# Scores of 16 of 24 attention pairs: stacked full-height matmuls in place of row-tiled ones, and one output tile fewer

## Chip, cores and metric

One core of one Trainium2 chip. The metric is the device time of one launch in microseconds; lower is better. The kernel before took 720.41 us (median of three runs, 712.51 to 721.36).

## What is computed

Softcapped attention over 4 batches of 12 heads, 448 positions of 64 features, and on its output, seen as 1792 tokens of 768 features, a two-layer network with the nonlinearity h - tanh(h). All in float32.

```python
scores = np.matmul(q, k.transpose(0, 1, 3, 2)) / np.sqrt(64)
scores = cap * np.tanh(scores / cap)
attn = softmax(scores)                       # over the last axis, 1e-9 in the denominator
x = np.matmul(attn, v).transpose(0, 2, 1, 3).reshape(4 * 448, 12 * 64)
h = x @ w_in                                 # 768 -> 2048
out = (h - np.tanh(h)) @ w_out               # 2048 -> 768
```

The kernel reads w_in and w_out as 64-bit words and decodes them on the chip.

## The kernel before

**Precision.** TensorE's fast format keeps fewer bits than float32. So most operands are split: a "hi" part, the value rounded by a cast to that format, and a "lo" part, the rest (`split`, L438: a cast on ACT or DVE, L432 or L434, then a subtraction on DVE, L443). A product takes three matmuls: hi by hi, hi by lo, lo by hi.

**Pairs.** Attention goes by pairs (b, p): two heads of a batch, one on partitions 0 to 63, the other on 64 to 127. There are 24 pairs, six a batch. `prep_pair` (L525) transposes the raw k and q to [128, 448] tiles kT and qT (L536), splits k into kst (hi in the first half of the columns, lo in the second), copies the tails of both heads into kt (L550, two copies of 64x128 in a tile whose other blocks are zero), and makes the hi and lo parts of q in qst (L557 on ACT, L562 on DVE).

**Scores.** `scores` (L668) runs four groups for a pair. The first is the tail: the last 64 keys of both heads as one 128-row block, three matmuls from kt. The other three take 128 keys of both heads: six matmuls on 64 rows each, alternating between the two heads and so between the two halves of the array's rows, into two PSUM banks (L616 in `qk_group`, L599). The bank tag "s" has two buffers; pairs 0 to 7 also use the accumulators' banks (`s_banks`, `FREE_PAIRS = 8`). ACT then takes tanh out of the bank (L626) and exp (L681). The products with v follow (`pv`, L742): eleven pairs in plain float32 (L760), thirteen in split form (L762, L763, L765), whose exponentials are split as well (L664, L657).

**Network.** `moe` (L1160) goes through segments (batch, first and last of 16 blocks of 128 hidden features): `first` (L1074, matmuls L1089 to L1091, 18 of 384 columns) gives h for a block, ACT and DVE make and split g, and `second` (L1120, L1142) adds its part to the output accumulators, three tiles of 128 tokens a batch, each three matmuls of 512 and three of 256 columns. Batches 0 and 1 are done in two segments each; between them the sums go to DRAM: `keep_y` (L1294) evicts three accumulators into tiles "o" and writes them; `store` (L1329) loads them into "o" tiles (L1336), adds the accumulator (L1317) and writes the output (L1360).

**Order.** All operations are entered into a planner (`Plan`), which gives each a cost and a due time and simulates the engines, buffers and DMA; its order is the order in which instructions are emitted, on every engine. Casts and plain copies (`copy`, L425) may go to ACT or DVE, as the planner finds. In the planner's prices a score group of two heads costs `GROUP = 3 * SCORE + 200.0`. Batch 0's scores come first by themselves (the lead); the scores of batches 1 to 3 are placed in between the MoE blocks of earlier batches (`SHARES`, `LEAD`).

**Names.** `sizes` (L379) gives the buffers of each tag: kst=2, kt=2, qst=2, kT=1, qT=1, o=3, s=2. Tiles made once and reused stand in `self.fixed` (L346), with their zeros written by POOL at the start.

Of the kernel before, what the change touches and what calls it, by code (L numbers as in the profile page):

```python
# [9 lines left out]
F32 = mybir.dt.float32  # L10
F32R = mybir.dt.float32r
# [28 lines left out]
FREE_PAIRS = 8  # L40

WARM = 18

BIAS, SWITCH = 1500.0, 80000.0
# [12 lines left out]

GROUP = 3 * SCORE + 200.0
SCORES = 3 * GROUP + 3 * SCORE

# [20 lines left out]
class Op:  # L81
    __slots__ = (
        "eng", "cost", "fn", "deps", "alloc", "later", "uses", "key", "due", "n", "succ", "need", "ready", "dma",
        "weight", "end",
    )


class Plan:
# [17 lines left out]

    def op(self, eng, cost, fn, deps=(), alloc=(), uses=(), key=1e18, dma=0.0, weight=1.0):
        o = Op()
        o.eng, o.cost, o.fn, o.due, o.dma, o.weight = eng, cost, fn, key, dma, weight
# [16 lines left out]
    def schedule(self, wait, bias):  # L126
# [57 lines left out]
        while left:  # L184
# [48 lines left out]
            for s in o.succ:  # L233
                s.ready = max(s.ready, o.end + self.latency(o, s))
                s.need -= 1
                if not s.need:
                    put(s)
# [73 lines left out]
class Build:  # L311
# [6 lines left out]
    def __init__(self, ctx, tc, q, k, v, w_in, w_out, out, consts, checks, general):  # L318
# [26 lines left out]

        self.fixed = {"kt": [], "vraw": []}  # L346
        for i in range(self.plan.tags["kt"]):
# [102 lines left out]

    def dma(self, eng, nbytes, fn, deps=(), alloc=(), uses=(), slow=1, long=False, key=1e18):
        c = (650.0 if long else 550.0) if eng == "SP" else 600.0
        return self.plan.op(eng, c, fn, deps, alloc, uses, key, dma=nbytes * slow / 360.0)

# [70 lines left out]
    def prep_pair(self, b, p):  # L525

        nc, S, D, F, TL, plan = self.nc, self.S, self.D, self.FULL, self.TAIL, self.plan
        T, tr = {}, {}  # L530
        for nm in ("k", "q"):
            raw, j, ops = self.raw_qk.pop((nm, b, p))
            t = T[nm] = plan.buf(nm + "T", [128, S])
            tr[nm] = self.dve(
                S,
                lambda t=t, raw=raw, j=j: nc.vector.transpose(t(), raw()[:, j].rearrange("p j a -> p (j a)")),  # L536
                ops, [t], [raw],
            )
        kst, kt, qst = plan.buf("kst", [128, 2, S], F32R), plan.buf("kt"), plan.buf("qst", [128, 2, S], F32R)
        kops = list(  # L540
            self.split(
                S, lambda: kst()[:, 0, :], lambda: kst()[:, 1, :], T["k"], [tr["k"]], ([kst], []),
                ([T["k"]], [kst, T["k"]]),
            )
        )
        tops = []
        for h, c0 in ((0, F), (1, 0)):
            rows = slice(D * h, D * h + D)
            tops.append(
                self.copy(  # L550
                    2 * TL, lambda h=h, rows=rows: kt()[rows, :, h, :],
                    lambda rows=rows, c0=c0: kst()[rows, :, c0 : c0 + TL].bitcast(F32), kops,
                    [] if h else [kt], [kst, kt] if h else [kst],
                )
            )
# [11 lines left out]
        self.ready[b, p] = dict(kst=kst, kt=kt, qst=qst, kops=kops, tops=tops, qops=[o1, o2])  # L567

    def prep_v(self, b, p):
# [12 lines left out]
    def s_banks(self, b, p, n):  # L582
# [12 lines left out]
        return out  # L595

    PRODUCTS = ((0, 0), (0, 1), (1, 0))

    def qk_group(self, b, p, c, dsts, e):  # L599

        nc, S, D = self.nc, self.S, self.D
        r = self.ready[b, p]
        heads = 2 if c < 3 else 1
        ps = self.s_banks(b, p, heads)

        def fn():
            qst = r["qst"]()
            for n, (i, j) in enumerate(self.PRODUCTS):
                for h in range(heads):
                    rows = slice(D * h, D * h + D) if heads == 2 else slice(0, 2 * D)  # L610
                    c0 = 128 * c + self.TAIL * h
                    if heads == 2:
                        k = r["kst"]()[rows, i, c0 : c0 + 128]
                    else:
                        k = r["kt"]()[:, i].rearrange("p a b -> p (a b)")
# [258 lines left out]
    def fetch_w(self, f):  # L874

        nc, DM, plan = self.nc, self.DM, self.plan
        if f in self.kept_op:
            u = plan.buf("u", [128, 2, DM])
            o = self.dma(
                "SP", 8 * 128 * DM, lambda: nc.sync.dma_start(out=u(), in_=self.u_kept[f]), [self.kept_op[f]], [u]  # L880
            )
            return u, [o]
        raw, ops = self.fetch_raw(f, key=EARLY_W[f] if f < len(EARLY_W) and not self.general else 1e18)
        u = plan.buf("u", [128, 2, DM])
# [7 lines left out]

    def fetch_raw(self, f, deps=(), key=1e18):

# [3 lines left out]
        for hp in range(2):  # L898

            def fn(hp=hp):  # L900
# [6 lines left out]
                self.dma(  # L907
                    "SP", 4 * 128 * DM, fn, deps, [] if ops else [raw], [raw] if ops else [], slow=1.75, long=True, key=key
                )
# [3 lines left out]
                "SP", 8 * 128 * DM, lambda: nc.sync.dma_start(out=raw()[:, 1, :], in_=self.w_out[cols, :]),  # L913
                deps, [], [raw], key=key,
            )
# [47 lines left out]
    def inspect(self, f):  # L963


        nc, n = self.nc, 2 * self.DM
        raw, ops = self.fetch_raw(f, [self.last_pe])
        x = lambda: self.word(raw, 1).bitcast(F32)
# [191 lines left out]
    def moe(self):  # L1160
# [37 lines left out]
        yield from self.rest()  # L1198

    def stash(self, f, g):  # L1200

# [6 lines left out]
        kept, o = self.kept_buf, 256 * (f % 3)  # L1208
        flat = lambda c: kept().rearrange("p a b -> p (a b)")[:, c : c + 128]
        ops = []  # L1210
# [10 lines left out]
    def rest(self):  # L1221
# [6 lines left out]
        for n, (fs, w, ops) in enumerate(groups):  # L1228

            def fn(n=n, fs=fs, w=w):  # L1230
                for j, f in enumerate(fs):
                    wh, wl = w(0)[:, 256 * j : 256 * j + 256], w(1)[:, 256 * j : 256 * j + 256]
                    kept, o, _ = self.kept[f]
                    a = kept().rearrange("p a b -> p (a b)")
                    gh, gl = a[:, o : o + 128], a[:, o + 128 : o + 256]
# [131 lines left out]
    def emit(self):  # L1367
# [118 lines left out]
```

## Time and profile before

| what | value |
|---|---|
| median of three runs | 720.41 us |
| the three runs | 721.36, 720.41, 712.51 us |
| the profiled execution | 707.93 us |
| its span, first to last instruction | 706.2 us |
| mean granted TensorE clock | 0.997 of 2.4 GHz |

Of the span, ACT is busy for 73%, DVE for 69%, TensorE's weight loads for 82%; instructions: 10301. In the profile PE is TensorE's matmuls, PEld its weight loads, DVE VectorE, ACT ScalarE, POOL GpSimd and SP the queue that issues most DMAs (SPq in rows). Tiles carry an "f" ahead of their names (fkst is kst). Matmuls are pipelined, so durations of neighbours overlap: what one costs is read from its start to the next one's start.

### The profile page before, as it was taken

To read this page: it belongs to the slowest core of one execution; us is meant where nothing else is said; L and a number is where in the kernel's file an instruction comes from. 1 tells how busy PE (TensorE), PEld (TensorE's weight loads), DVE (VectorE), ACT (ScalarE), POOL (GpSimd) and SP (SyncE) were. 2 spreads that over 40 slices of the span, in tenths; PEclk is the share of its full clock that TensorE was granted. 3 is DMA by queue.
4 is the path that set the end of the run, shared out by engine and by line. 5 is a ranking of instruction groups with operands and counts; after the bars stand their busy time and mean duration, and the time that the engine had idled before them with its cause. 6 is when DMAs were issued, how large, how long until landed. Compare 5 with 4: busy or idle time off the path is not lost.

```text
span 706.2 us, 10301 instructions
## 1 busy us (share of the span) xinstructions
PE 691.7 (98%) x3768; PEld 576.1 (82%) x3768; DVE 489.2 (69%) x752; ACT 514.5 (73%) x898; POOL 27.1 (4%) x57
## 2 busy tenths in 40 slices
PE   7999999999999999999999999999999999999996
PEld 5555677777788988788898888888889999999996
DVE  3789999888788599999659878676783333243331
ACT  5999766778888497888359798889876555455553
POOL 1011100000300000000000000000000000000000
PEclk9999999999999999999999999999999999999999
DMA  7999999999976239996966876766558455566523
GB/s 107 157 256 258 280 231 278 248 208 237 307 220 158 100 105 276 292 266 187 316 242 199 241 194 148 199 180 198 173 143 282 129 146 142 179 179 146 146 68 116
DMA packets 162878, 140.12 MB, mean 198 GB/s; under 512 B 116228, under 2 KB 146052, under 8 KB 162820
## 3 DMA queue, kind: packets, MB, share of 16 engines
q1 hardware_dynamic: 158900, 122.02, 68.7%
q0 software_dynamic: 3840, 17.30, 6.6%
q8 instruction: 31, 0.51, 0.3%
q14 instruction: 27, 0.22, 0.1%
q10 hardware_dynamic: 80, 0.07, 0.0%
HBM read 114.20 MB, written 25.17 MB: 197 GB/s over the span
## 4 chain that ended last, share of the span: by engine, by line
PE 79%; DMA 11%; SPq 4%; ACT 3%; DVE 2%; issue 1%; DVEq 0%; ACTq 0%
PE facc L1142 25%; PE fh L1089 10%; PE fh L1091 10%; PE fh L1090 10%; PE fs L760 6%; PE fs L616 6%; DMA fu<-fuk 4%; PE fs L1142 3%; DMA fw<-in_moe_w_in_dram 2%; SPq L483 2%; DMA fkraw<-in_k_dram 2%; PE fs L762 2%; PE fs L763 2%; PE facc L616 2%; PE fs L765 2%; DMA fxl<-fxk 1%
## 5 line engine op out<-in xcount | busy, mean ns | idle before, releaser
L1142 PE MATMUL facc<-fwo,fgh 128*128 128x512 f32 (+1 forms) x768 | 169.4, 342 | 0.0
L1142 PEld LDWEIGHTS facc<-fwo,fgh 128*128 128x128 f32 x768 | 123.2, 188 | 23.1 <-issue 9.1
L1089 PE MATMUL fh<-fxh,fwi 128*128 128x384 f32 x384 | 134.6, 351 | 0.9 <-DVE fg L1104 0.9
L1091 PE MATMUL fh<-fxh,fwi 128*128 128x384 f32 x384 | 129.9, 338 | 0.4 <-DVE fwi L443 0.4
L1090 PE MATMUL fh<-fxl,fwi 128*128 128x384 f32 x384 | 129.0, 336 | 0.8 <-DMA fxl<-fxk 0.7
L443 DVE TENSOR_TENSOR fwi<-fu,fwi 128x768 fp32r<-128x768 f32 x66 | 62.8, 951 | 57.7 <-ACT fwi L432 57.5
L1142 PE MATMUL facc<-fwo,fgl 128*128 128x512 f32 (+1 forms) x384 | 98.8, 338 | 0.0
L432 ACT CAST fwi<-fu 128x768 fp32r<-128x768 f32 x61 | 50.9, 835 | 53.9 <-PE fh L1091 39.8
L1089 PEld LDWEIGHTS fh<-fxh,fwi 128*128 128x128 f32 x384 | 72.1, 188 | 12.5 <-issue 7.4
L1090 PEld LDWEIGHTS fh<-fxl,fwi 128*128 128x128 f32 x384 | 72.2, 188 | 3.0 <-DMA fxl<-fxk 1.6
L1091 PEld LDWEIGHTS fh<-fxh,fwi 128*128 128x128 f32 x384 | 72.0, 187 | 0.7 <-DVE fwi L443 0.7
L443 DVE TENSOR_TENSOR fwo<-fu,fwo 128x768 fp32r<-128x768 f32 x66 | 62.6, 951 | 12.6 <-ACT fwo L432 12.3
L1104 DVE TENSOR_TENSOR fg<-fh,fg 128x384 f32<-128x384 f32 x64 | 35.5, 555 | 50.7 <-ACT fg L1102 49.9
L1142 PEld LDWEIGHTS facc<-fwo,fgl 128*128 128x128 f32 x384 | 58.7, 188 | 8.4
L1102 ACT ACTIVATE fg<-fh 128x384 f32<-128x384 f32 x64 | 31.3, 490 | 43.6 <-PE fh L1091 43.3
L432 ACT CAST fwo<-fu 128x768 fp32r<-128x768 f32 x58 | 48.0, 831 | 12.2 <-PE facc L1142 11.9
L626 ACT ACTIVATE fe<-fs 128x448 f32<-128x448 f32 x91 | 45.1, 542 | 7.5 <-PE fs L616 7.4
L443 DVE TENSOR_TENSOR fel<-fe,feh 128x896 fp32r<-128x896 f32 x39 | 42.4, 1089 | 11.8 <-ACT feh L432 11.6
L432 ACT CAST feh<-fe 128x896 fp32r<-128x896 f32 (+1 forms) x63 | 49.1, 786 | 1.4 <-PE fs L763 0.7
L681 ACT ACTIVATE fe<-fe,absc 128x896 f32<-128x896 f32 (+1 forms) x52 | 49.4, 955 | 0.5
L616 PE MATMUL fs<-fqst,fkst 64*128 64x448 f32 x309 | 47.9, 398 | 0.4 <-DVE fsumT L792 0.4
L443 DVE TENSOR_TENSOR fgl<-fg,fgh 128x384 fp32r<-128x384 f32 x64 | 35.4, 554 | 15.8 <-ACT fgh L432 15.6
(172 smaller groups left out, 1193.1 us busy)
## 6 DMA issues: line engine op xcount, KB each, us to landing
fu<-fuk SPq DMA_DIRECT2D x48, 768.0 KB
fw<-in_moe_w_in_dram SPq DMA_DIRECT2D x64, 384.0 KB
fw<-in_moe_w_out_dram SPq DMA_DIRECT2D x32, 768.0 KB
fuk<-fu POOLq DMA_DIRECT2D x16, 768.0 KB, 6.1
fqraw<-in_q_dram SPq DMA_DIRECT2D x44, 112.0 KB
fkraw<-in_k_dram SPq DMA_DIRECT2D x44, 112.0 KB
out_dram<-fo SPq DMA_DIRECT2D x12, 384.0 KB
fvraw<-in_v_dram SPq DMA_DIRECT2D x26, 96.0 KB
```

Of the source, the lines that this page charges most:

```text
L432: self.nc.scalar.copy(out(), in_())
L443: lambda: self.nc.vector.tensor_sub(lo(), x(), hi().bitcast(F32)),
L616: nc.tensor.matmul(ps[h]()[:, :S], k, qst[rows, j, :], start=n == 0, stop=n == 2)
L626: S, lambda h=h: nc.scalar.activation(dsts[h](), ps[h]()[:, :S], AF.Tanh), [o],
L681: lambda e=e, w=w: nc.scalar.activation(e()[:, :w, :], e()[:, :w, :], AF.Exp, scale=self.absc),
L760: nc.tensor.matmul(out, va, e, start=n == 0, stop=n == 3)
L1089: nc.tensor.matmul(h()[:, :n], wh, ah, start=(d == 0), stop=False)
L1090: nc.tensor.matmul(h()[:, :n], wh, al, start=False, stop=False)
L1091: nc.tensor.matmul(h()[:, :n], wl, ah, start=False, stop=(d == ND - 1))
L1102: n, lambda: nc.scalar.activation(g()[:, :n], h()[:, :n], AF.Tanh), [prev], [g], [h], psum=True, key=k
L1104: o = self.dve(n, lambda: nc.vector.tensor_sub(g()[:, :n], h()[:, :n], g()[:, :n]), [o], [], [g, h], key=k + 600)
L1142: nc.tensor.matmul(banks[bk]()[:, c0 : c0 + ne], lhs()[:, ts], w()[:, k, e0 : e0 + ne], start=bk in firsts and bk not in begun, stop=stop ...
```

## The change

For the first eight pairs (`TILED_PAIRS = 8`) the scores stay as they were. For the other 16, `stack_pair` lays out the operands so that a matmul uses all 128 rows: k of a head with its hi part on one half of the partitions and its lo part on the other (kst), q's hi part copied onto both halves (qst, one slot for each head), so that one matmul gives hi by hi and lo by hi. A second one multiplies kz, the head's k on its own half and zeros on the other, with ql, the lo part of q of both heads. So a head's block of 128 keys takes two full-height matmuls into one bank, and the tail three for both heads. kst has a gap of 64 zero columns between its halves, and kst and kz become fixed tiles whose zeros are written once. "o" has two buffers in place of three, kt one in place of two; ql is new. The planner's `GROUP` goes up by 200, and the cost of a stacked pair is 15 SCORE in its shares. Operations get a field `lag`, which is 0.0 in all uses (left out below).

```diff
+TILED_PAIRS = 8
+INSPECT_LAG, RAW_LAG, KEPT_LAG = 0.0, 0.0, 0.0
-GROUP = 3 * SCORE + 200.0
+GROUP = 3 * SCORE + 400.0
...
-        self.fixed = {"kt": [], "vraw": []}
+        self.fixed = {"kst": [], "kz": [], "kt": [], "vraw": []}
+        S = self.S
+        for i in range(self.plan.tags["kst"]):
+            t = self.cst.tile([128, 2 * S + self.TAIL], F32R, name=f"{nm}kst{i}")
+            nc.gpsimd.memset(t.bitcast(F32)[:, S : S + self.TAIL], 0.0)
+            self.fixed["kst"].append(t)
+        for i in range(self.plan.tags["kz"]):
+            t = self.cst.tile([128, 2 * S], F32R, name=f"{nm}kz{i}")
+            nc.gpsimd.memset(t.bitcast(F32)[D:, 0:S], 0.0)
+            nc.gpsimd.memset(t.bitcast(F32)[:D, S:], 0.0)
+            self.fixed["kz"].append(t)
...
-        n = dict(kraw=2, qraw=2, kT=1, qT=1, kst=2, kt=2, qst=2, vraw=1, v1=2, v2=2, e=2, eh=4, el=3)
+        n = dict(kraw=2, qraw=2, kT=1, qT=1, kst=2, kz=2, ql=2, kt=1, qst=2, vraw=1, v1=2, v2=2, e=2, eh=4, el=3)
...
-        n.update(g=1, gh=2, gl=2, o=3, s=2, h=1, acc0=1, acc1=1, acc2=1, acc3=1, acc4=1)
+        n.update(g=1, gh=2, gl=2, o=2, s=2, h=1, acc0=1, acc1=1, acc2=1, acc3=1, acc4=1)
...
+        if not self.tiled(b, p):
+            return self.stack_pair(b, p, T, tr)
...
+    def tiled(self, b, p):
+        return b * self.NP + p < TILED_PAIRS
...
+    def stack_pair(self, b, p, T, tr):
+        nc, S, D, TL, plan = self.nc, self.S, self.D, self.TAIL, self.plan
+        half = (slice(0, D), slice(D, 2 * D))
+        kst, kz = plan.buf("kst"), plan.buf("kz")
+        kops, zops = [], []
+        def part(rows, hp):
+            return (kst()[:, S + TL :] if hp else kst()[:, 0:S])[rows]
+        for hp in range(2):
+            rows, other = half[hp], half[1 - hp]
+            o1, o2 = self.split(
+                S,
+                lambda hp=hp, rows=rows: part(rows, hp),
+                lambda hp=hp, other=other: part(other, hp),
+                lambda rows=rows: T["k"]()[rows],
+                [tr["k"]] + kops[:1],
...
+            o2.cost += SHIFT
...
+            zops.append(
+                self.copy(
+                    S, lambda hp=hp, rows=rows: kz()[rows, S * hp : S * hp + S], lambda rows=rows: T["k"]()[rows],
+                    [tr["k"]], [] if hp else [kz], [T["k"]] + [kz] * hp,
+                )
+            )
+        qst, ql = plan.buf("qst", [128, 2, S], F32R), plan.buf("ql", [128, S], F32R)
+        def move(to, of, at, deps):
+            return self.copy(
+                S, lambda: qst()[half[to], at, :], lambda: qst()[half[of[0]], of[1], :].bitcast(F32), deps, [], [qst],
+                shift=to != of[0],
+            )
+        o1 = self.act(
+            S, lambda: nc.scalar.activation(qst()[:, 0, :], T["q"](), AF.Copy, scale=self.s8), [tr["q"]],
+            [qst], [T["q"]], aps=1,
+        )
+        lo = self.dve(
+            S,
+            lambda: nc.vector.scalar_tensor_tensor(
+                ql(), T["q"](), self.s8, qst()[:, 0, :].bitcast(F32), op0=ALU.mult, op1=ALU.subtract
+            ),
+            [o1], [ql], [qst, T["q"]], extra=60,
+        )
+        b1, b2 = move(1, (1, 0), 1, [o1]), move(0, (1, 0), 1, [o1])
+        a2 = move(1, (0, 0), 0, [o1, b1, b2, lo])
...
+    def stacked_block(self, b, p, hp, c, e, dst):
...
+        ps = self.plan.buf("s")
+        heads = (0, 1) if c == 3 else (hp,)
+        passes = len(heads) + 1
+        def block(t, h):
+            if c == 3:
+                return t[:, S : S + 2 * TL] if h else t[:, F : F + 2 * TL]
+            return (t[:, -F:] if h else t[:, 0:F])[:, 128 * c : 128 * c + 128]
+        def fn():
+            kst, qst, kz, ql = r["kst"](), r["qst"](), r["kz"](), r["ql"]()
+            todo = [(block(kst, h), qst[:, h, :]) for h in heads]
+            todo.append((block(kz, 0 if c == 3 else hp), ql))
+            for n, (k, q) in enumerate(todo):
+                nc.tensor.matmul(ps()[:, :S], k, q, start=n == 0, stop=n == passes - 1)
...
+        if not self.tiled(b, p):
+            made = [self.stacked_block(b, p, h, c, e, dsts[h]) for h in range(heads)]
+            return [t for ts, _ in made for t in ts], sum(cost for _, cost in made)
...
-            share[b] = NP * SCORES + f32 * 8 * FULL32 + (NP - f32) * 22 * SCORE
+            share[b] = sum(SCORES if self.tiled(b, p) else 15 * SCORE for p in range(NP)) + f32 * 8 * FULL32 + (NP - f32) * 22 * SCORE
```

## Rows read from the trace of the kernel before

**Rows 1.** The page's first part: busy us, share of the span, instructions.

```profile
PE 691.7 (98%) x3768; PEld 576.1 (82%) x3768; DVE 489.2 (69%) x752; ACT 514.5 (73%) x898; POOL 27.1 (4%) x57
```

**Rows 2.** Windows by stage: length, busy us by engine, granted clock, DMA share, GB/s.

```profile
85.00:185.00 100.00, 100.00 (x493) 75.35 (x493) 87.24 (x118) 73.31 (x130) 9.56 (x18) 1.00 1.07 248
185.00:265.00 80.00, 78.68 (x442) 67.81 (x441) 64.20 (x96) 61.02 (x107) 2.58 (x5) 1.00 0.54 164
265.00:345.00 80.00, 79.07 (x433) 66.56 (x431) 72.87 (x97) 60.51 (x105) 2.67 (x5) 1.00 0.98 265
345.00:515.00 170.00, 169.78 (x944) 147.17 (x945) 125.32 (x196) 141.50 (x231) 0.00 (x0) 1.00 0.71 203
```

**Rows 3.** Waits of PE: who for whom, us in all, times, longest.

```profile
PE fs L616 <- ACT fe L626: 1.3, 1, 1.3
```

**Rows 4.** Timeline of PE around two row-tiled groups: start, us, what.

```profile
105.01 0.34 PE L1090 MATMUL fh<-fxl,fwi 128*128 128x384 f32 x1
...
106.77 0.34 PE L1091 MATMUL fh<-fxh,fwi 128*128 128x384 f32 x1
107.03 0.87 PE L616 MATMUL fs<-fqst,fkst 64*128 64x448 f32 x6
107.84 0.44 PE L1089 MATMUL fh<-fxh,fwi 128*128 128x384 f32 x1
108.11 0.34 PE L1090 MATMUL fh<-fxl,fwi 128*128 128x384 f32 x1
...
374.49 0.87 PE L1142 MATMUL facc<-fwo,fgh 128*128 128x512 f32 x4
...
377.61 0.86 PE L1142 MATMUL facc<-fwo,fgh 128*128 128x512 f32 x4
```

**Rows 5.** Timeline of PE, a tail block and the next line.

```profile
94.06 0.77 PE L616 MATMUL fs<-fqst,fkt 128*128 128x448 f32 x3
94.67 0.85 PE L1142 MATMUL facc<-fwo,fgh 128*128 128x512 f32 x4
```

**Rows 6.** Groups by line and form: busy us, mean ns, idle before.

```profile
L432 ACT CAST fkst<-fkT 128x448 fp32r<-128x448 f32 x14 | 8.0, 569 | 1.5 <-DVE fkT L536 1.5
L434 DVE CAST fkst<-fkT 128x448 fp32r<-128x448 f32 x10 | 3.9, 386 | 2.7 <-PE facc L616 2.1 <-PE fs L616 0.5
L443 DVE TENSOR_TENSOR fkst<-fkT,fkst 128x448 fp32r<-128x448 f32 x24 | 14.8, 618 | 2.9 <-ACT fkst L432 2.7
L432 ACT CAST fkt<-fkst 64x128 fp32r<-64x128 f32 x42 | 12.4, 296 | 1.4 <-DVE fkst L443 1.0
L432 ACT CAST feh<-fe 64x448 fp32r<-64x448 f32 x26 | 14.6, 563 | 0.5
L657 DVE TENSOR_TENSOR feh<-fe,feh 64x448 fp32r<-64x448 f32 x26 | 16.1, 620 | 8.5 <-ACT feh L432 7.9
```

**Rows 7.** Windows of 20 us, columns as in the windows by stage.

```profile
60.00:80.00 20.00, 19.07 (x81) 11.72 (x81) 19.84 (x32) 17.54 (x33) 3.89 (x8) 1.00 1.06 272
300.00:320.00 20.00, 20.00 (x112) 16.98 (x112) 19.72 (x27) 17.63 (x31) 1.07 (x2) 1.00 0.88 242
```

**Rows 8.** Output tiles: two of the timeline, one of the chain, one DMA landing.

```profile
340.45 1.02 DVE L1317 TENSOR_TENSOR fo<-facc,fo 128x512 f32<-128x512 f32 x2 [0.93 <-PE facc L1142]
340.75 2.28 SPq L1360 DMA_DIRECT2D out_dram<-fo  x1
...
348.28 3.13 PE facc L1142 x18
...
fuk<-fu POOLq DMA_DIRECT2D x16, 768.0 KB, 6.1
```

**Rows 9.** Timeline of the start: a memset on POOL, the first tail copies.

```profile
1.71 0.53 POOL L408 MEMSET fv1float<- 128x512 f32 x1
...
9.22 0.61 ACT L432 CAST fkt<-fkst 64x128 fp32r<-64x128 f32 x2 [0.69 <-DVE fkst L443]
```

More of the change, by code (lines that the diff above doesn't have):

```diff
@@ L83 @@
         "eng", "cost", "fn", "deps", "alloc", "later", "uses", "key", "due", "n", "succ", "need", "ready", "dma",
-        "weight", "end",
+        "weight", "end", "lag",
     )
@@ L105, in buf, with op @@
         return b
-    def op(self, eng, cost, fn, deps=(), alloc=(), uses=(), key=1e18, dma=0.0, weight=1.0):
+    def op(self, eng, cost, fn, deps=(), alloc=(), uses=(), key=1e18, dma=0.0, weight=1.0, lag=0.0):
         o = Op()
-        o.eng, o.cost, o.fn, o.due, o.dma, o.weight = eng, cost, fn, key, dma, weight
+        o.eng, o.cost, o.fn, o.due, o.dma, o.weight, o.lag = eng, cost, fn, key, dma, weight, lag
         o.deps = [d for d in deps if d is not None]
@@ L233, in schedule @@
             for s in o.succ:
-                s.ready = max(s.ready, o.end + self.latency(o, s))
+                s.ready = max(s.ready, o.end + o.lag + self.latency(o, s))
                 s.need -= 1
@@ L551, in prep_pair @@
                     2 * TL, lambda h=h, rows=rows: kt()[rows, :, h, :],
-                    lambda rows=rows, c0=c0: kst()[rows, :, c0 : c0 + TL].bitcast(F32), kops,
+                    lambda rows=rows, c0=c0: self.pieces(kst(), rows, c0), kops,
                     [] if h else [kt], [kst, kt] if h else [kst],
@@ L567, in prep_pair, with pieces @@
         self.ready[b, p] = dict(kst=kst, kt=kt, qst=qst, kops=kops, tops=tops, qops=[o1, o2])
+    def tiled(self, b, p):
+        return b * self.NP + p < TILED_PAIRS
+    def pieces(self, kst, rows, c0):
+        S, TL = self.S, self.TAIL
+        t = kst[rows, c0 : c0 + S + 2 * TL].bitcast(F32)
+        return t.rearrange("p (a b) -> p a b", b=TL)[:, 0 : S // TL + 2 : S // TL + 1, :]
+    def stack_pair(self, b, p, T, tr):
[13 more added lines that the diff above has]
+                [tr["k"]] + kops[:1],
+                ([] if kops else [kst], []),
+                ([kst, T["k"]] if kops else [T["k"]], [kst, T["k"]]),
+            )
+            o2.cost += SHIFT
+            o2.fn = lambda hp=hp, rows=rows, other=other: nc.vector.tensor_sub(
+                part(other, hp), T["k"]()[rows], part(rows, hp).bitcast(F32)
+            )
+            kops += [o1, o2]
+            zops.append(
[13 more added lines that the diff above has]
+            [qst], [T["q"]], aps=1,
+        )
+        lo = self.dve(
[4 more added lines that the diff above has]
+            [o1], [ql], [qst, T["q"]], extra=60,
+        )
+        b1, b2 = move(1, (1, 0), 1, [o1]), move(0, (1, 0), 1, [o1])
+        a2 = move(1, (0, 0), 0, [o1, b1, b2, lo])
+        qops = [[o1, a2], [b1, b2]]
+        self.ready[b, p] = dict(kst=kst, kops=kops, kz=kz, zops=zops, qst=qst, qops=qops, ql=ql, lops=[lo])
@@ L595, in s_banks @@
         return out
+    def stacked_block(self, b, p, hp, c, e, dst):
+        nc, S, F, TL = self.nc, self.S, self.FULL, self.TAIL
+        r = self.ready[b, p]
+        ps = self.plan.buf("s")
[11 more added lines that the diff above has]
+                nc.tensor.matmul(ps()[:, :S], k, q, start=n == 0, stop=n == passes - 1)
+        deps = [o for h in heads for o in r["kops"][2 * h : 2 * h + 2] + r["qops"][h]]
+        deps += [r["zops"][h] for h in heads] + r["lops"]
+        cost = SCORE * passes
+        o = self.pe(cost, fn, deps, [ps], [r["kst"], r["qst"], r["kz"], r["ql"]])
+        new = e.users == 0
+        t = self.act(
+            S, lambda: nc.scalar.activation(dst(), ps()[:, :S], AF.Tanh), [o],
+            [e] if new else [], [ps] if new else [ps, e], psum=True, key=self.at + cost + 400,
+        )
+        return [t], cost
     PRODUCTS = ((0, 0), (0, 1), (1, 0))
@@ L612, in fn @@
                     if heads == 2:
-                        k = r["kst"]()[rows, i, c0 : c0 + 128]
+                        k = r["kst"]()[rows, (S + self.TAIL) * i + c0 : (S + self.TAIL) * i + c0 + 128]
                     else:
@@ L879, in fetch_w @@
             o = self.dma(
-                "SP", 8 * 128 * DM, lambda: nc.sync.dma_start(out=u(), in_=self.u_kept[f]), [self.kept_op[f]], [u]
+                "SP", 8 * 128 * DM, lambda: nc.sync.dma_start(out=u(), in_=self.u_kept[f]), [self.kept_op[f]], [u],
+                lag=KEPT_LAG,
             )
             return u, [o]
-        raw, ops = self.fetch_raw(f, key=EARLY_W[f] if f < len(EARLY_W) and not self.general else 1e18)
+        raw, ops = self.fetch_raw(
+            f, key=EARLY_W[f] if f < len(EARLY_W) and not self.general else 1e18, lag=RAW_LAG
+        )
         u = plan.buf("u", [128, 2, DM])
```

23 lines of the change are left out of this document (13 added, 10 removed).

## Prediction

> **What bounds the kernel now.** I read the busy shares first: TensorE (PE) is busy 691.7 of 706.2 us [rows 1], so there is hardly any idle time to win back, and the next question is where the other engines stand. The windows by stage [rows 2] cut out the 430 us from 85 to 515, in which batches 1 to 3 are scored in between the MoE matmuls and in which all that changes lies: PE is busy in 427.5 of them (100.00, 78.68, 79.07 and 169.78), at a granted clock of 1.00, that is 2.4 GHz throughout. DVE is busy for 349.6 and ACT for 336.3, together 686 of 860, or 80%. So the stage is as long as its matmuls, and a microsecond taken from PE's work is a microsecond of the end, as long as ACT and DVE keep up. The list of waits [rows 3] says the same: the score matmuls waited for tanh (L626) 1.3 us in all, once. A busy PE says nothing of how well it is used, though, so the third view is the timeline of PE, read from start to start [rows 4, 5].
>
> **The tiled groups, and what replaces them.** One of the 64-row groups (six matmuls, two heads in two row halves) starts at 107.03, and the next line at 107.84: 0.81. It has edges too. Ten steps of the MoE matmuls ahead of it, 105.01 to 106.77, take 0.176 each; the last one takes 0.26 to the group, 0.08 more, and the first one behind takes 0.27 (107.84 to 108.11), 0.09 more: 0.99 us in all [rows 4]. A second group, between two L1142 blocks, gives 1.03: from 374.49 to 377.61 it is 3.12, less two blocks of 1.04 (a third of the 3.13 of the chain's row) [rows 4, 8]. I take 1.00. All pairs from the ninth on have such groups, 16 pairs of 3, so 48.
>
> The replacement is four 128-row matmuls of 448 columns for a group. Before has such matmuls: the tail block at 94.06 is three of them over 128 rows, with the same moving width, and the next line starts 0.61 later [rows 5], 0.203 each, with no extra at either side. Four make 0.81. The tail stays at three. The saving is 1.00 - 0.81 = 0.19 us a group, times 48 = **9.1 us**. That these matmuls start freely behind each other follows from the tail block, which sums three in one bank as the new code does. Each new block also asks for one "s" bank in place of two, so up to 1.3 us of the wait on tanh can go as well [rows 3]; I take none of it and keep it for the range.
>
> Here the Trainium skill speaks against the change. The rows above show 0.81 between starts and 1.00 in all for six half-height matmuls. TensorEngine Tiling (Array Packing), section Theoretical Speedup, gives up to twofold for a contraction of 64 rows; by that a group is three matmul times, 0.61, and the change would add 0.20 a group, 9.6 us in all. The trace does not bear that out for a group of six among full-height work. The same page, section Key Properties, says that a change of tiling mode drains the engine; the 0.2 at the two edges and the 0.2 inside the group agree with that.
>
> **The preparation.** A stacked pair needs its operands copied across the halves, and that goes to ACT and DVE [rows 6]. Before, a pair takes one cast of k (0.569 on ACT, 0.386 on DVE), one subtraction (0.618) and two tail copies (0.296 each): 1.78 us. After: two half-height casts of k (nearest row 0.563, the 64x448 cast of e), two subtractions that write to the other half (0.620, the row of L657, which does just that; the shift costs nothing beside 0.618), two copies into kz (0.563 each) and three moves of q (0.563 each): 5.18. The activation and the subtraction that make the two parts of q stand on both sides. That is 3.40 more for a pair, 54.4 us for 16. If all seven casts and copies went to DVE at 0.386 it would be 3.94 against 1.60, 37 us in all. I take 54, since all 26 half-height casts of before were on ACT.
>
> With it ACT and DVE have 740 us of work in a stage of 421 us, 88% of the two; in 85 to 345, where ten of the pairs lie, 419 + 34 = 453 of 509, 89%. What does that cost PE? Bounds: from 300 to 320 the two were busy 37.35 of 40 us and PE lost nothing; from 60 to 80 they were busy 37.38 of 40 and PE lost 0.93 us of 20, 4.7% [rows 7]. So between 0 and, at 4.7% of the 254 us, 12 us. I take 3, nearer the lower end, because 300 to 320 has the same mix (scores among MoE blocks) and 60 to 80 is the end of the lead. The cover is the distance between pairs: a pair is prepared once in some 27 us (430 by 16), with two buffers each of kst, kz, ql and qst. If that cover is gone, what comes late is the tail block of the next pair, and behind it on PE's queue all MoE blocks.
>
> **Two output tiles.** Where a segment ends on sums kept in DRAM, the third tile's load has to wait until the first tile's write has landed. At the first such end the write is issued at 340.75, and the third accumulator is wanted again by the third of the blocks that start at 348.28 and take 3.13, so at 350.4 [rows 8]. Lower bound: 0.39 MB at the 265 GB/s of that stage is 1.5 us each way, and the two additions take 1.02 [rows 2, 8]: ready at 344.8, free of cost. Upper bound: 6.1 us to landing, as for POOL's 768 KB [rows 8], each way: 354.0, 3.6 us late. There are two such ends, so 0 to 7.2; I take 1. SP's queue holds the weight loads behind that load, which is why it isn't nothing. Where tiles are written only, the third eviction is late by one write, and there PE has other blocks to run.
>
> **Free edits.** The memsets of kst and kz go ahead of the others on POOL. A 128x512 one takes 0.53 us, so four of 64x448 and two small ones add some 2 us; they are done well before the first tail copy at 9.22 [rows 9]. If that cover were gone the start would be late by as much. One kt buffer: only the first eight pairs use it, once each. The lags are zero. The planner's higher price for a tiled group moves due times and with them the order of all queues; I price it at nothing, with 3 us to either side, since PE has so little idle time in the stage to win or to lose by order alone [rows 2].
>
> **The sum.** -9.1 + 3 + 1 = -5.1 us. The profiled execution took 707.93, so 702.8, a ratio of 0.993. The median of the runs, 720.41, is 1.018 times that execution, and the runs lie from 712.51 to 721.36; the same ratio gives 715.2, and I forecast **715**. Times below are on that scale.
>
> **Rivals.**
> *All of the preparation is covered* (25 in 100). For it: PE lost nothing at 93% [rows 7]. Then -9.1, or -10.4 with the wait on tanh: 711 to 710.
> *ACT and DVE become the bound* (17 in 100), on the other side. Place: 85 to 515, worst in 85 to 345. Their 740 us take 430 us, as long as before, if the two can be kept at 86.1% on average; below that the kernel is slower. At 85% the stage takes 435.5, +5.5: 713.4, or 726. For it: the casts and subtractions alternate between the two engines, and DVE is at 87% of 85 to 185 already [rows 2]. Against it: the 93% of [rows 7].
> *The third output tile is late at both kept ends* (6 in 100): -9.1 + 3 + 7.2 = +1.1, 722. Against it: the planner may put other blocks there.
> *The tiles do run at twice the rate* (3 in 100): a group would cost 0.61 in place of 0.81 for four full matmuls, and the change adds 9.6: 717.5, or 730. Against it: the 0.81 and the edges of [rows 4]; for it only that two groups of 48 were read. This is the rule of the Trainium skill, TensorEngine Tiling (Array Packing), section Theoretical Speedup.
>
> **How the numbers follow.** My forecast, a net of -3 to -7 us (713 to 717), has 45 in 100; the rest, 4, is an order of the queues that none of these describes. For 8 in 10 the range takes in the covered case with the low end of the runs (712.51 is 1.1% below the median: 710 becomes 702) and on the other side the late tile and part of the bound engines: 701 to 724. About 2% is what a measurement of this kernel can tell from no change. Faster by over 2% (below 706) needs 14 us, more than all of the PE saving; only the covered case with a fortunate order or a low median gets there: 0.13. Slower by over 2% (above 735) needs ACT and DVE below some 83%, or the twofold tiles and a wait: 0.05. Within 2%: 0.82.
>
> **What would show it.** In the profile after: no 64-row matmul behind the eighth pair; the new line's matmuls 0.20 apart with no step at either edge; 16 times 15 of them. ACT and DVE together busy by 37 to 54 us more, most of it in 85 to 345, with casts moving to DVE. PE's waits, if any, on ACT's copies of q or on tanh; if the sum of those is over 9 us, the third paragraph was wrong. A wait of L1142 on the output tiles shows the late tile. A PE that waits for nothing and a saving of under 5 us would mean that the group's price was misread.

## The result, and the profile after

The changed kernel takes 720.88 us (median of 20 runs) where the kernel before, run beside it, takes 716.68: a ratio of **1.0098**, 95% interval 1.0071 to 1.0124. The ratio is taken from fast runs alone (one run of the changed kernel, 841.98 us, is left out as slow), so it is not the quotient of the two medians, which is 1.0059. Forecast was 0.993. The time lies inside the range that was given, but by either figure the kernel became slower, not faster. The profiled execution took 720.03 us, span 718.3. That of before, 707.93, was a lucky one: the lowest of 20 runs of before is 709.34.

First, the matmuls. The timeline of PE in the changed kernel, a stacked group among MoE matmuls (start, us, what):

```profile
462.91 0.34 PE L1215 MATMUL fh<-fxh,fwi 128*128 128x384 f32 x1
463.09 0.36 PE L701 MATMUL fs<-fqst,fkst 128*128 128x448 f32 x1
463.29 0.37 PE L701 MATMUL fs<-fql,fkz 128*128 128x448 f32 x1
463.50 0.37 PE L701 MATMUL fs<-fqst,fkst 128*128 128x448 f32 x1
463.70 0.36 PE L701 MATMUL fs<-fql,fkz 128*128 128x448 f32 x1
463.90 0.33 PE L1213 MATMUL fh<-fxh,fwi 128*128 128x384 f32 x1
464.08 0.34 PE L1214 MATMUL fh<-fxl,fwi 128*128 128x384 f32 x1
```

Four steps of 0.20, 0.81 in all, and no extra step at either edge (0.18 into the group, 0.18 behind the next matmul): just what [rows 5] promised. Over all 240 stacked matmuls the median step is 0.203. So the work is saved. To see where it went, I split PE's time from the traces: every matmul's step to the next one's start, against the step that the same shape takes undisturbed (0.175 us for 384 columns, 0.203 for 448, 0.231 for 512, 0.1175 for 256, 0.3755 for a float32 one, 1.00 for a row-tiled group with its edges, which is also the median of the 49 of them behind 85 us in the trace of before). The undisturbed steps sum to the *work*; the rest, waits and stretches of low clock, is *lost*. Work fell from 683.4 to 674.4 us, by 9.0 (a count of matmuls times these steps). Lost time rose from 15.0 to 36.0.

The windows of the changed kernel by stage (length, busy us of PE, PEld, DVE, ACT, POOL, granted clock, DMA share, GB/s), to be held against [rows 2]:

```profile
0.00:85.00 85.00, 76.08 (x298) 43.60 (x299) 68.31 (x127) 66.87 (x119) 12.87 (x33) 0.98 0.96 205
85.00:185.00 100.00, 97.36 (x446) 75.36 (x445) 90.36 (x126) 83.18 (x143) 4.79 (x9) 1.00 1.04 231
185.00:265.00 80.00, 79.82 (x436) 72.28 (x435) 64.39 (x99) 67.50 (x115) 6.42 (x12) 1.00 0.57 170
265.00:345.00 80.00, 77.65 (x416) 68.72 (x415) 77.37 (x101) 67.74 (x117) 3.36 (x6) 1.00 0.88 256
```

PE has lost its full stretches: 97.36 of 100 us where it had 100.00, 77.65 of 80 where it had 79.07. The loss begins in the lead, before any stacked pair (the first stacked matmul starts at 102.0): PE is busy for 76.08 of the first 85 us, and in the kernel before for 79.93:

```profile
0.00:85.00 85.00, 79.93 (x323) 47.80 (x324) 67.21 (x124) 73.45 (x132) 11.92 (x29) 0.98 1.00 208
```

The three largest waits of the changed kernel from 20 to 120 (who for whom, us in all, times, longest) are those of row-tiled and float32 blocks; stacked blocks (L701) add 1.9 near its end:

```profile
PE fs L736 <- ACT fnum L448: 1.9, 1, 1.9
PE fs L880 <- DMA fv1float<-in_v_dram: 1.7, 1, 1.7
PE fs L736 <- DVE fsumT L912: 1.1, 2, 0.6
```

L736 is the row-tiled group of the first eight pairs; the change leaves its matmuls as they were and raises its price in the planner. In the trace of before the same stretch has two waits:

```profile
PE fs L760 <- ACT feh L626: 0.5, 1, 0.5
PE fs L616 <- DVE fsumT L792: 0.4, 1, 0.4
```

### The profile page after: what moved, and what is told of

Its sections match the earlier page's. It is cut to its first block, busy times and chain, and to the rows that moved or that the text cites. A ratio compares the mean times of both kernels' runs of the same rounds, so it can differ in the third digit from the quotient of the medians.

```text
span 718.3 us, 10235 instructions
## 1 busy us (share of the span) xinstructions
PE 691.0 (96%) x3672; PEld 589.4 (82%) x3672; DVE 511.5 (71%) x796; ACT 543.1 (76%) x934; POOL 27.8 (4%) x61
## 4 chain that ended last, share of the span: by engine, by line
PE 58%; ACT 14%; DVE 13%; DMA 9%; issue 3%; SPq 2%; DVEq 0%; ACTq 0%
PE facc L1266 18%; PE fh L1213 8%; PE fh L1215 8%; PE fh L1214 7%; PE fs L880 5%; PE fs L701 4%; PE fs L1266 3%; DMA fu<-fuk 3%; DMA fw<-in_moe_w_in_dram 3%; DMA fw<-in_moe_w_out_dram 2%; ACT fe L709 2%; ACT fe L801 2%; ACT feh L448 2%; ACT fwi L448 2%; DVE fsumT L912 1%
## 5 line engine op out<-in xcount | busy, mean ns | idle before, releaser
L1266 PEld LDWEIGHTS facc<-fwo,fgh 128*128 128x128 f32 x768 | 126.1, 188 | 19.5 <-issue 3.0
L709 ACT ACTIVATE fe<-fs 128x448 f32<-128x448 f32 x91 | 47.0, 544 | 7.5 <-PE fs L701 4.0
L701 PE MATMUL fs<-fqst,fkst 128*128 128x448 f32 x128 | 46.5, 383 | 4.6 <-DVE fsumT L912 1.3
L448 ACT CAST fwo<-fu 128x768 fp32r<-128x768 f32 x55 | 45.6, 832 | 5.2 <-PE facc L1266 3.2
```

What stands on the lines that cost most here:

```text
L448: self.nc.scalar.copy(out(), in_())
L701: nc.tensor.matmul(ps()[:, :S], k, q, start=n == 0, stop=n == passes - 1)
L709: S, lambda: nc.scalar.activation(dst(), ps()[:, :S], AF.Tanh), [o],
L1266: nc.tensor.matmul(banks[bk]()[:, c0 : c0 + ne], lhs()[:, ts], w()[:, k, e0 : e0 + ne], start=bk in firsts and bk not in begun, stop=stop ...
```

## The experiments

Each run was timed against the kernel before on its own chip, where before had medians from 716.3 to 718.9 us. The table has the ratio with its 95% interval, PE's work, and PE's lost time by stretch in the profiled execution (the last column has also what lies ahead of 20 and behind 560, 5 to 10 us). Single executions of one kernel differ by 12 us and more, so the ratio decides and the lost time only shows places; the profiled execution's time stands beside the median for that. Quotients of medians lie up to 0.4% from the ratios, so smaller differences are not read.

| run | ratio | interval | median | profiled | work | lost 20-85 | 85-265 | 265-400 | 400-560 | lost in all |
|---|---|---|---|---|---|---|---|---|---|---|
| before | 1 | | 716.7 | 707.9 | 683.4 | -0.5 | 2.3 | 3.3 | 2.7 | 15.0 |
| changed | 1.0098 | 1.0071-1.0124 | 720.9 | 720.0 | 674.4 | 6.9 | 6.3 | 8.5 | 8.1 | 36.0 |
| e1 changed, old price | 0.9992 | 0.9960-1.0023 | 718.7 | 721.8 | 674.4 | 1.4 | 8.6 | 11.8 | 8.5 | 37.8 |
| e2 before, new price | 1.0148 | 1.0100-1.0196 | 729.3 | 731.4 | 683.4 | 5.8 | 8.1 | 7.8 | 6.9 | 38.6 |
| e3 before, two o | 1.0023 | 0.9990-1.0055 | 720.0 | 720.9 | 683.4 | -0.4 | 5.1 | 9.4 | 5.2 | 27.7 |
| e4 changed, three o, one kz | 1.0032 | 0.9993-1.0071 | 719.9 | 718.9 | 674.4 | 6.6 | 4.2 | 6.8 | 9.4 | 35.0 |
| e5 e4 with old price | 1.0025 | 0.9982-1.0067 | 717.8 | 715.7 | 674.4 | -0.6 | 9.0 | 6.7 | 10.0 | 31.8 |
| e6 e1 without stacking | 1.0020 | 0.9979-1.0062 | 719.7 | 723.0 | 683.4 | 1.1 | 6.6 | 9.5 | 5.4 | 30.1 |
| e7 e1 without preparation | 1.0010 | 0.9975-1.0045 | 715.8 | 715.9 | 674.4 | 4.8 | 5.6 | 5.0 | 9.6 | 31.6 |
| e8 before, price in the matmul alone | 1.0080 | 1.0049-1.0110 | 722.5 | 721.5 | 683.4 | 2.6 | 3.8 | 9.4 | 5.0 | 28.4 |
| e9 e5, stacked blocks underpriced | 0.9981 | 0.9945-1.0017 | 716.6 | 716.8 | 674.4 | 0.6 | 5.2 | 10.0 | 10.2 | 32.9 |
| e10 before, price + 0 | 0.9873 | 0.9828-0.9918 | 710.8 | 710.5 | 683.4 | 1.1 | 0.9 | 7.7 | 0.5 | 17.5 |
| e11 e5, all prices -3% | 0.9876 | 0.9825-0.9927 | 709.0 | 704.8 | 674.4 | 0.2 | 3.0 | 5.8 | 5.1 | 20.8 |
| e12 before, all prices -3% | 0.9849 | 0.9800-0.9897 | 707.9 | 705.4 | 683.4 | 1.9 | 1.2 | 1.7 | 1.7 | 12.3 |
| e13 e11 and e9 together | 0.9912 | 0.9880-0.9945 | 708.7 | 711.7 | 674.4 | 2.9 | 3.0 | 11.6 | 3.1 | 27.6 |
| e14 e13, two o, two kz | 0.9892 | 0.9851-0.9932 | 707.0 | 716.1 | 674.4 | 3.7 | 3.7 | 9.9 | 6.9 | 32.0 |
| e15 before, all prices -6% | 0.9911 | 0.9876-0.9947 | 709.1 | 710.5 | 683.4 | 4.4 | 0.4 | 4.9 | 0.9 | 17.6 |
| e16 e13 without preparation | 0.9897 | 0.9863-0.9930 | 706.6 | 705.6 | 674.4 | -0.1 | 2.8 | 9.6 | 2.0 | 21.2 |
| e17 e11, one decode pass less | 0.9887 | 0.9827-0.9947 | 707.6 | 709.0 | 674.4 | 1.5 | 11.8 | 2.3 | 4.0 | 25.1 |
| e18 e12, one decode pass less | 0.9893 | 0.9840-0.9946 | 707.7 | 703.8 | 683.4 | -0.5 | 0.6 | 1.9 | 1.6 | 10.7 |

### The planner's price

e1, the changed kernel:

```diff
-GROUP = 3 * SCORE + 400.0
+GROUP = 3 * SCORE + 200.0
```

> The changed kernel with the planner's old price of a row-tiled group (GROUP with + 200.0 in place of + 400.0), all else as changed. Theory A (the new price reorders the lead and that is the loss): the seventh MoE block (step 6), which starts at 136.9 us before and at 150.6 after, starts near 137 again, and the kernel takes 10 to 14 us less than the changed one, ratio to before 0.99 to 1.00. Theory B (the stacking itself, its preparation and buffers, delays the lead and its end): step 6 stays near 150 and the ratio at 1.01.

e2, the kernel before:

```diff
-GROUP = 3 * SCORE + 200.0
+GROUP = 3 * SCORE + 400.0
```

> The kernel before with the new price of a row-tiled group alone (+ 400.0). Theory A: step 6 moves from 136.9 to some 150 us and the kernel is 10 to 14 us slower, ratio 1.014 to 1.02. Theory B: step 6 stays within 3 us of 136.9 and the ratio within 0.997 to 1.004.

One constant, which puts no instruction anywhere, makes the kernel before 1.5% slower, and taking it back makes the changed one 1.06% faster (1.0098 to 0.9992; 0.6% by the medians). Theory A holds for the ratio, though e1's gain of 7.6 us is less than the 10 to 14 that it gave. It missed a detail: in e1 the seventh MoE block starts at 146.3, not near 137. By the trace the products with v of one more pair (6.0 us) stand ahead of it, and 10.3 us are lost up to there in place of 6.0. The lead itself is mended (lost 1.4 in place of 6.9), but e7, also at the old price, lost 4.8 there in its profile, 2.7 of it in one wait for a load of v. The three largest waits of PE in e2 from 20 to 120, the first of the same kind as in the changed kernel:

```profile
PE fs L616 <- ACT fnum L432: 2.4, 1, 2.4
PE fh L1089 <- DVE fg L1104: 1.9, 1, 1.9
PE fs L616 <- ACT fel L626: 0.9, 1, 0.9
```

e8 splits the constant's two uses in the kernel before, the simulated time and the due times:

```diff
-        o = self.pe(cost, fn, r["kops" if heads == 2 else "tops"] + r["qops"], ps, [r[ks], r["qst"]])
+        o = self.pe(cost + 200.0 * (heads == 2), fn, r["kops" if heads == 2 else "tops"] + r["qops"], ps, [r[ks], r["qst"]])
```

> The kernel before with the new price in the planner's simulated matmul time alone; the due times, which are summed from the same constant, stay as before. Theory: it is the due times that move the first MoE block ahead of the lead's end (60.6 us before, 54.7 after): then this kernel stays at a ratio of 1.00 with the first MoE block near 60. Rival (the simulated time itself reorders the lead): ratio 1.015 as with the whole price, first MoE block near 55.

Neither theory: 1.008, and the first MoE block at 63.4. About half of the loss comes with the simulated time alone. The other half needs the due times as well; these were not run by themselves.

### Output tiles

e3, the kernel before, and e4, the changed one:

```diff
-o=3, s=2
+o=2, s=2
```

> The kernel before with two output tiles in place of three, nothing else. Theory C (the third tile late): steps 24 to 32, 61.1 us before and 65.2 after, take 64 to 66 us, an eviction wait of some 2 us comes up at the end of the third-last segment near 540, and the ratio is 1.005 to 1.01. Rival (two tiles cost nothing, the loss of that stretch is ACT's and DVE's): 61 us and a ratio within 0.998 to 1.002.

```diff
-kst=2, kz=2, ql=2, kt=1
+kst=2, kz=1, ql=2, kt=1
...
-o=2, s=2
+o=3, s=2
```

> The changed kernel with three output tiles again and, for room, one kz tile in place of two. Theory C: steps 24 to 32 fall from 65.2 towards 61 us, the wait of PE on the eviction at 548 goes, 4 to 7 us less than the changed kernel. Rival: no gain, and the single kz adds a wait of the tail block on its copies of up to 1 us a pair in 15 pairs. Step 6 stays near 150 by theory A, since the price is the new one.

e3's 1.0023 can't be told from no change; e4 is 0.66% under the changed kernel (0.45% by the medians). The stretch of steps 24 to 32 came as theory C said, 66.0 us in e3 and 61.9 in e4. The late tile is there in the traces. In e3 it is at the first end with kept sums, where the prediction looked for it: the third tile's load is issued at 351.92, behind the first tile's write at 348.03, its addition starts at 360.48 where before has 340.45 [rows 8], and PE waits for it (start, us, engine, what, idle before and releaser):

```profile
360.48 1.01 DVE L1317 TENSOR_TENSOR fo<-facc,fo 128x512 f32<-128x512 f32 x2
361.21 1.07 PE L1142 MATMUL facc<-fwo,fgh 128*128 128x512 f32 x4 [2.16 <-DVE fo L1317]
```

In the changed kernel it is at another place, the end of the third-last segment, where tiles are only written:

```profile
547.94 0.58 ACT L448 COPY fo<-facc 128x512 f32<-128x512 f32 x1 [0.47 <-DMA out_dram<-fo]
...
548.57 1.46 PE L1266 MATMUL facc<-fwo,fgh 128*128 128x512 f32 x4 [1.89 <-ACT fo L448]
```

The third eviction waits for the first tile's write, and PE waits 1.89 us for the eviction. e4 has no such wait; with one kz it loses more from 400 to 560 instead (9.4).

### Do the parts add, and what is the stacking worth?

e5 joins e1 and e4:

```diff
-GROUP = 3 * SCORE + 400.0
+GROUP = 3 * SCORE + 200.0
-kst=2, kz=2, ql=2, kt=1
+kst=2, kz=1, ql=2, kt=1
-o=2, s=2
+o=3, s=2
```

> The changed kernel with the old price (+ 200.0), three output tiles and one kz tile: stacking almost alone. If the parts add (the old price is worth 1.06% of the time, the third tile 0.66%), the ratio to before is 0.993, that is 5 us less than before. Rival: every edit redraws the order and the parts do not add; then the ratio lies between 0.997 and 1.004, as e1 and e4 do singly.

e6 is e1 with

```diff
-TILED_PAIRS = 8
+TILED_PAIRS = 24
```

> The changed kernel with the old price and no stacking (all 24 pairs row-tiled); two output tiles and one tail-key tile stay. It is the partner of e1 without the stacking. If the stacking keeps its 9 us of PE work, this one is 1.2% slower than e1 (ratio 1.011); if preparation eats it, it lies within 0.4% of e1 and close to e3 (ratio 1.000 to 1.004).

The parts don't add: 1.0025. Against e4 (1.0032) the old price alone changes nothing here, so what the price costs depends on the rest of the order. And e6 without the stacking is only 0.28% over e1 with it, less than the intervals; of 9.0 us some 2 are left. e7 asks whether the preparation eats them:

```diff
-            zops.append(
...
-        b1, b2 = move(1, (1, 0), 1, [o1]), move(0, (1, 0), 1, [o1])
-        a2 = move(1, (0, 0), 0, [o1, b1, b2, lo])
-        qops = [[o1, a2], [b1, b2]]
+        qops = [[o1], [o1]]
```

> e1 without the two copies into kz and the three moves of q (left out; the halves that they fill stay zero, so a part of the scores is not computed). PE's work is that of e1, 674 us; ACT and DVE have 45 us less. If the preparation on ACT and DVE causes e1's waits, PE's lost time from 85 to 560, 28.8 us in e1's profile, falls to 10 or less and the ratio to 0.985 to 0.99. Rival (the waits come of the order and of two output tiles, whatever ACT and DVE carry): ratio 0.996 to 1.0.

The time does not say so: 1.0010 against 0.9992. ACT's busy time from 85 to 560 falls from 395 to 370 us (over the whole span ACT and DVE have 39 us less, not 45). PE's lost time there falls from 28.9 to 20.2 us in the profiles, where a cause in this load would have left 10 or less. The windows 85 to 560 of e1 and then of e7:

```profile
85.00:560.00 475.00, 459.33 (x2403) 402.76 (x2402) 388.98 (x573) 395.44 (x664) 14.78 (x27) 0.99 0.78 212
```

```profile
85.00:560.00 475.00, 462.59 (x2449) 406.39 (x2448) 384.31 (x557) 370.31 (x617) 14.97 (x28) 1.00 0.79 216
```

### A theory of margin

So far everything that was touched got slower or stayed. That could be because any edit draws a new order (R), or because of the price itself (M): a price below the real one lets the planner believe that PE is fast, and it then orders the feeding work of ACT, DVE and the DMA queues early against PE; the old price was 0.81 for a group that takes 1.00 [rows 4], the new one and that of the stacked blocks are true, with nothing to spare. M says that lower prices help even the kernel before.

e9, on e5, and e10, on the kernel before:

```diff
-        o = self.pe(cost, fn, deps, [ps], [r["kst"], r["qst"], r["kz"], r["ql"]])
+        o = self.pe(cost - 94.0 * (c < 3), fn, deps, [ps], [r["kst"], r["qst"], r["kz"], r["ql"]])
```

> e5 (stacking, old price, three output tiles, one kz tile) with each stacked block of 128 keys priced 94 ns under its 408 in the planner, so that a stacked group is as much too cheap in the plan as a row-tiled group is at the old price (188 of 1000). Theory M (a price below the real one makes the planner put the feeding work of ACT, DVE and the DMA queues early against PE, and that margin is what the stacked blocks, priced truly, lost): ratio to before 0.985 to 0.993, PE's lost time under 27 us. Rival R (any edit redraws the order, and the order of before was picked by its constants): ratio 0.998 to 1.006, as all stacked versions so far.

```diff
-GROUP = 3 * SCORE + 200.0
+GROUP = 3 * SCORE
```

> The kernel before with the row-tiled group priced still lower (+ 0.0 in place of + 200.0, measured 1.00 us against a price of 0.61). Theory M: the margin grows, ratio 0.990 to 1.000. Rival R: 1.002 to 1.015, like the other edits of before.

e11, on e5, and e12, on the kernel before (the price of a float32 product, `FULL32`, stays):

```diff
-COLS = {256: 118.0, 384: 175.5, 448: 204.0, 512: 233.0}
+COLS = {256: 114.5, 384: 170.2, 448: 197.9, 512: 226.0}
```

> e5 with all matmul prices of the planner 3% lower (about 20 us less PE time in the plan, spread over the whole kernel). Theory M: PE's lost time falls to 15 to 25 us and the ratio to 0.980 to 0.990, faster than both kernels. Rival R: 0.998 to 1.006.

> The kernel before with the same 3% off all matmul prices. Theory M: ratio 0.988 to 0.998, and the distance to e11 is the 9.0 us of PE work (1.25%). Rival R: 1.002 to 1.010.

M's forecast of a faster kernel came in three of the four: e10, e11 and e12 are 1.2 to 1.5% faster than the kernel before, with intervals well clear of 1; e9 is a miss (0.9981). R, which forecast 0.998 or more, falls for these. M missed sizes too: e10 and e12 gained more than it forecast, and e11 does not lie the 1.25% under e12 that it forecast. What remains of PE's waits in e12 from 85 to 560:

```profile
PE fh L1089 <- DVE frb L1104: 0.9, 1, 0.9
PE fh L1091 <- DVE fwi L443: 0.5, 1, 0.5
PE fh L1090 <- DVE fxl L443: 0.2, 1, 0.2
```

That the feeding work stands earlier in the order is argued from how the planner works, and the traces do not bear it out for the one feeder counted here: the subtraction that completes a block's w_in (L443 into fwi) ends a median of 9.9 us ahead of the block's first matmul in before, 8.4 in e12 and 10.4 in e2 (first 40 blocks), so later, not earlier, at the low price. Shown is that the price alone moves the time; how it does so stays open. e12 is faster than both kernels by an edit of four constants. e15 asks for how far this goes:

```diff
-COLS = {256: 118.0, 384: 175.5, 448: 204.0, 512: 233.0}
+COLS = {256: 111.0, 384: 165.0, 448: 191.8, 512: 219.0}
```

> The kernel before with all matmul prices 6% lower in place of the 3% of e12. Theory M: more margin has little left to give, PE's lost time is 19 us in e12's profile and 10 of them are the two ends; ratio 0.980 to 0.988. Rival: too low a price starves PE the other way (it is planned to wait for what is early), 0.990 to 1.0.

0.9911, as the rival said: no further, perhaps back; 3% was enough. (The 19 us of lost time that this expectation gives for e12 are 12.3 as the table counts.)

### Why the stacking still brings nothing

e11 has 9.0 us less PE work than e12 and is no faster. e13 is e11 with e9's edit, e14 the same with the buffers of the change (o=2, kz=2), e16 is e13 with the lines of e7 left out.

> e11 with each stacked block also priced 94 ns lower, so that the stacked groups have the margin that a row-tiled group has in e12 (about 0.2 us a group beside the 3%). Theory M: with equal margins the 9.0 us of PE work show, ratio to before 0.972 to 0.980, 6 to 9 us under e12. Rival W (what eats the 9 us is no question of margin: preparation, the single kz or the banks): 0.983 to 0.990, level with e11 and e12.

> e13 with the buffers of the change itself (two output tiles, two kz). If the single kz is what e11 loses from 400 to 515 (5.0 us there, 2.8 in the changed kernel), that stretch falls to 2 us or less, and the late third output tile shows instead near 345 to 400 and 515 to 560. Theory M: ratio 0.975 to 0.985. Rival W: 0.985 to 0.995.

> e13 without the two copies into kz and the three moves of q (left out, their halves stay zero, so a part of the scores is not computed): 45 us less on ACT and DVE. If preparation is what remains of the loss, this is 4 to 9 us faster than e13; if it was covered, within 2 us of e13.

All three lie from 0.989 to 0.991: theory M's 0.972 to 0.980 for e13 is refuted, rival W (it is no question of margin) stands, and the single kz and the preparation are not the cause either. e17 and e18 take a pass of the weight decoding off DVE, in e11 and in e12:

```diff
-        o = self.dve(
+        return self.dve(
...
-        return self.dve(
-            n,
-            lambda: nc.vector.scalar_tensor_tensor(
-                ui(), self.word(raw, 0), 29, ui(), op0=ALU.logical_shift_right, op1=ALU.bitwise_or
-            ),
-            [o], [], [u, raw],
-        )
```

> e11 (stacking with margin) without the third pass of the weight decoding on DVE (16 instructions of 1.75 us, 28 us; the three lowest mantissa bits of the weights are left out). From 265 to 345 DVE is busy for 77.0 of 80 us in e11. Theory D (there and from 85 to 185 DVE is the bound, so what the stacking takes from PE turns into waits for DVE): PE's lost time from 85 to 345, 8.1 us in e11's profile, falls to 3 or less, and e17 is 5 to 8 us faster than e11 and 5 to 9 us faster than e18. Rival (single waits of an order that the planner did not foresee, on no engine in particular): e17 within 3 us of e11 and of e18.

> e12 (row-tiled with margin) without the same pass of the decoding. Theory D: it has little to gain, since PE lost only 2.8 us from 85 to 345 in e12's profile: 0 to 3 us faster than e12. Rival: the same as e17 within 3 us.

Theory D falls: 707.6 and 707.7, level again. From 265 to 400 the lost time does fall as D said (5.8 to 2.3), but from 85 to 265 it rises from 3.0 to 11.8. (e17's profiled execution lies 1.4 us above its median and e18's 4.0 below, so part of the difference between the two profiles is that.) The waits of PE from 85 to 560 in e17:

```profile
PE fs L701 <- ACT fnum L448: 5.3, 4, 2.9
PE fs L701 <- ACT fe L709: 2.6, 1, 2.6
PE fs L701 <- ACT fel L709: 0.8, 1, 0.8
```

and in e18:

```profile
PE fh L1082 <- DVE frb L1097: 0.7, 1, 0.7
PE fh L1083 <- DMA fxl<-fxk: 0.3, 1, 0.3
```

In e17 the stacked blocks (L701) wait for what frees an "s" bank: the copy fnum, which empties a bank of the products with v, and tanh. The same kind leads in e11 (fnum) and in e1 (the transpose fsumT, which reads such a bank):

```profile
PE fs L701 <- ACT fnum L448: 2.7, 4, 1.5
PE fs L701 <- DVE fsumT L912: 6.1, 6, 3.1
```

The other traces agree. Counting from 85 to 560 PE's waits into an s bank that ended with an instruction that reads one, e12, e15 and e18 have none, and the stacked versions with lower matmul prices have 3.8 us (e11), 5.2 to 5.7 (e13, e14, e16) and 9.6 (e17). At the old or the new price it is 1.3 in before and 3.3 to 5.8 in the other row-tiled runs (e10, priced lower still, 1.1), and 5.1 to 10.9 in the stacked ones. These two banks serve all scores from the ninth pair on and all products with v. It is the best candidate for the bound behind the 9 us, but it is not shown: the kernel gives five PSUM tiles to accumulators, two to s and one to h, and a third s in place of one of the others was not tried.

## Why the prediction was wrong

**The PE saving: right.** 9.1 us forecast, 9.0 in the work. The steps at the edges, the 0.20 between stacked matmuls and their count came as said.

**The twofold rate: there inside a group, but not for the group.** In the trace of before the six matmuls of a group start two by two, 3 ns apart, and the steps from one two to the next and out of the group are 0.306, 0.199 and 0.287 us (medians). So the middle step has the twofold rate, 0.199 for two matmuls of half height against 0.203 for one of full height, and the other two steps and the edges, 0.09 and 0.10, lose it again: 1.00 in all against 0.81 for four stacked matmuls. The Trainium skill, TensorEngine Tiling (Array Packing), section Theoretical Speedup, gives twofold as an upper bound ("Up to 2×"); the estimate of 0.61 for a group that the prediction drew from it does not come out here.

**The preparation: its size right, its price not what mattered.** DVE and ACT are busy for 22.3 and 28.6 us more, 51 in all, between the bounds of 37 and 54. But e7 and e16, with 39 and 42 us less on the two engines, differ from e1 and e13 by less than the intervals (0.18% slower, 0.15% faster). The 3 us that I charged stand for something that costs more (some 7 of the 9 us: e1 against e6) and that is neither this load nor DVE's decoding.

**Free edits: the step that failed.** "I price it at nothing, with 3 us to either side" was the planner's price, and the reason given, that PE has little idle time to win or lose by order alone, does not carry: little idle time in one profile leaves much to lose. e2 shows 1.48% (10.6 us of 717), e1 1.06% (7.6), both well over the 3 us, though on top of e4 the same price is worth nothing (e5); and e12, with 1.5% the other way, shows that there was time to win as well. What happened lies in the 4 in 100 that the prediction left to "an order of the queues that none of these describes". That 720.88 lies inside 701 to 724 is luck: those bounds were drawn for other causes. An order written by a simulation is part of the kernel, and a constant of it is not a comment. That this constant was closer to the truth than the old one should have raised the question what the untruth had been good for.

**Two output tiles: mechanism right, places partly, size low.** I looked at the two ends with kept sums and waved the ends that only write ("there PE has other blocks to run"). In the changed kernel the wait came up at one of these, 1.89 us at 548; in e3 at the first kept end, 2.16 us at 361; in e1 where sums are first written away, 1.79 us at 303. Within 2 us behind each the clock goes to its lower level for 3.4 us, which costs up to 1.7 us more, so that one late tile cost up to 3.5 to 3.9 us where I took 1 for all. As a whole it is 0 to 0.7% (e3, e4, which changes kz as well).

**The base.** I scaled one execution to the median. That execution had lost 15.0 us; the median is 8.8 us above it. Of 122 further executions of before, timed beside the experiments, none is under 709.67 us and the median granted clock is 0.992, where the profiled one had 0.997. So the picture of a PE with hardly a wait in [rows 3] is of an untypical execution, and it made the plan look safer than it is.

Of the rivals, "ACT and DVE become the bound" came nearest on the side (slower), but not as a mechanism: the loss begins in the lead, where no pair is stacked, and lifting load off either engine did not help.

**Open.** Why stacked and row-tiled versions end level at every margin and load that was tried (e1 and e6, e11 and e12, e17 and e18), as if the 9.0 us were given back in waits each time. The waits point to the two s banks; no run separates this from an order that the planner draws less well for single-bank blocks. Open too is how a price moves the time.

## What to carry to other kernels

When an order is made by a planner, ask of every edit what it does to the planner's beliefs, and test its constants singly: here one price was worth more than the whole rearrangement of the matmuls. Prices of the bottleneck engine that are a few per cent too low (3% here, 6% was no better) gave 1.5% by another order of the same work; a truer price is not by itself a better one. Judge a base by several runs: one profiled execution can lie 9 us from the median.

## What the hardware showed that I had not expected

A wait of PE can cost more than its length. Behind the 1.89 us at 548 the granted clock is at its lower level, 1.2 GHz, for the next 3.4 us (windows of the changed kernel):

```profile
544.00:548.80 4.80, 2.91 (x19) 2.39 (x18) 0.91 (x3) 4.29 (x6) 0.00 (x0) 1.00 0.56 223
548.80:552.20 3.40, 3.40 (x12) 3.10 (x12) 1.76 (x4) 1.01 (x4) 0.00 (x0) 0.50 0.46 54
552.20:556.00 3.80, 3.80 (x23) 3.58 (x22) 0.56 (x1) 0.74 (x2) 0.00 (x0) 0.99 0.93 327
```

Matmuls of 384 columns step by 0.32 there (550.47, 550.79, 551.11, 551.43) in place of 0.175, so the stretch costs 1.7 us beside the wait. e1 has three such stretches, the first behind a wait of 3.1 us for a bank, at 168; the profiled execution of before has none between 20 and 700. Waits of 1.65 and 1.87 us in the lead of the changed kernel were not followed by one, nor was one of 2.96 in e6, at 536.
